# Six softmax exponentials and a transpose, issued half a slot earlier in an attention and soft-MoE kernel

## The chip, the cores and the metric

The kernel runs on one core of a Trainium2 chip. The metric is device time in microseconds. Before the change the median of three runs is 294.74 us (294.28 to 294.95).

## The reference, cut to what matters

Attention over 8 batches, 12 heads, 448 tokens and head dimension 64, with a one more in the denominator than softmax has (the term `exp(-m)`); then a soft mixture of experts over all 3584 tokens: 32 slots (8 experts of 4), each slot an average of the tokens (softmax down the tokens, "dispatch"), two dense layers, and each token a mixture of the slots (softmax along the slots, "combine").

```python
scores = scale * np.matmul(q, k.transpose(0, 1, 3, 2))
e = np.exp(scores - m)                              # m: maximum of the row
x = (e / (e.sum(-1) + np.exp(-m) + 1e-09)) @ v      # then 3584 x 768
logits = x @ phi                                    # 3584 x 32
d = softmax(logits, axis=0); slot_input = d.T @ x
c = softmax(logits, axis=1)
out = c @ experts(slot_input)
```

## The kernel before, in words

The kernel is written out by hand: each engine runs its instructions in the order of the program, and waits on semaphores of the others. The attention runs over 48 pairs of heads (six to a batch). The main loop (L766) has one **slot** s for a pair, in two halves, y = 0 and y = 1. In a slot the engines do this, for different pairs ahead of and behind s:

- Scores for the row maxima: PE L308 into PSUM (`ps_a`, pool psA of 3 buffers), DVE L309 reduces each one (617 ns); a last, shorter one is L325 and L327.
- Scores again, transposed, with the maxima added as a bias by a second matmul: PE L368 and L371 (`ps_b`, pool psB of 4 buffers), ACT L373 takes the exponentials; the shorter last one is L397, L400 and L403.
- The product with v, L437, twelve matmuls in each half and eight more in y = 0 (`ps_av`, one buffer); ACT L450 copies it out; DVE L468 adds up the denominator and L474 inverts it; POOL L478, L488 and L489 multiply.
- PX (L503): x of pair s-2 is turned by PE L510 into `ps_x` (psB), and ACT L516 casts it to xT. This is at the end of y = 1.
- The turns of q and k six slots ahead (L282, `ps_t` in psB and psA), copied out by ACT L286 (or DVE L286) and DVE L287. Every third slot the maxima are turned (`ps_m`) and copied by ACT L343 to `mT`.
- POOL also issues most loads (q: L176, k: L179, v: L183 and L184, expert weights: L113), and copies v into shape (V: L409 to L412, every third slot).

When a batch b is through the attention, its logits and both softmaxes are worked in between, in six steps that `P(b)` (L525) returns; each batch from the second on also rescales the sums of those before it by `corr`. The steps run in chosen halves of later slots: `post` (L672) maps a half slot 2s+y to what is issued there, after that half's AV matmuls and ahead of PX. For batches 0 to 5 (`late`, L521) with base half slot 2(6b+8):

- step 0: logits (L544), copy (L567), maximum (L571); step 1: transpose (L579), maximum (L581), `c_sub` on POOL (L586); step 2: new maximum (L592, L594) and `d_sub` on POOL (L600). These are in half slots 0, 1 and 2.
- step 3: `exps` on ACT (L605) out of `z` that `c_sub` and `d_sub` wrote, and `corr`: an exponential on ACT (L610) and the rescaling of `acc` on POOL (L616); batch 0 has no L610 and L616.
- step 4: `c_turn`, the combine weights turned by PE (L636, into `ps_ct` of psA) and copied by DVE (L637).
- step 5: `s_mm` and `s_add` (L632, L641), the dispatch sums.

Before the change steps 3, 4 and 5 are in half slots 4, 5 and 9. The half slots 2 and 3 are those of slot 6b+9, called the cast's slot in the prediction, whose L516 is the cast in question; 4 and 5 are those of slot 6b+10.

Of the kernel before, what the change touches and what calls it, by code (L numbers as in the profile page):

```python
# [31 lines left out]
def kernel(  # L32
# [123 lines left out]
    with ExitStack() as at:  # L156
# [364 lines left out]
        late = lambda b: b < B - 2  # L521
# [150 lines left out]
        post = {}  # L672
        for b in range(B - 1):
            for z, f in enumerate(P(b)):
                at_z = (0, 1, 2, 4, 5, 9) if late(b) else (0, 1, 2, 3, 4, 6)
                post.setdefault(2 * (PB * b + PB + 2) + at_z[z], []).append(f)

        ub = ubuf.rearrange("p n c -> p (n c)").bitcast(BF16)
# [371 lines left out]
```

## Time and profile before

| | |
|---|---|
| median of 3 runs | 294.74 us |
| profiled execution | 293.25 us |
| its span (first to last instruction) | 291.5 us |
| mean granted TensorE clock | 0.959 |
| step 3 to step 3, batches 3 to 4 and 4 to 5 | 28.23 us |
| DMA | 58.67 MB, 201 GB/s over the span |

A line of a timeline reads: start in us, length in us, engine, line of the kernel, operation, tile written <- tiles read, shapes, and how many instructions are merged. An entry in brackets is the idle time of the engine before it and what ended it. ACT's and DVE's records overlap by some 0.1 us when the engine is fed without a gap, so what an instruction costs is the time from its start to the next one's. A line of the page's groups reads: line, engine, operation, tiles, count | busy us, mean ns | idle before it and what ended most of it.

The attention's main loop fills the span from 60 to 236 us; the last batch, the experts and the output follow.

### The profile page before, as it was taken

Reading aid. Unit: us, or ns where it says so; the run is one execution under the profiler, and the core shown is the slowest. Engines: PE = TensorE matmul, PEld = TensorE weight load, DVE = VectorE, ACT = ScalarE, POOL = GpSimd, SP = SyncE. Lnnn points to the kernel's source line nnn. Section 1 sums busy time; section 2 is a strip of 40 time slices with the busy share of each in tenths; the row PEclk is TensorE's granted clock in tenths of the full one; section 3 lists DMA queues with packets and bytes.
Section 4 is the critical chain, followed back from the end, with each engine's and each line's share of the span. In section 5 each row is a group of like instructions: output and inputs, shape, how many; then the busy total and the mean of one; then the engine's idle time right before and its main releaser. Section 6 shows DMA issues by size and latency. Waiting matters only on the chain.

```text
span 291.5 us, 12388 instructions
## 1 busy us (share of the span) xinstructions
PE 266.0 (91%) x5191; PEld 153.7 (53%) x5191; DVE 248.2 (85%) x604; ACT 249.1 (85%) x555; POOL 189.6 (65%) x349
## 2 busy tenths in 40 slices
PE   5999899999999989999999999999999999996820
PEld 4545555555665545656655665566555556662100
DVE  5999899999999988999999999999999575437940
ACT  4569999999999989999999999999999987337820
POOL 8672897878787988798779878996785633000000
PEclk9999999999999999999999999999999999998555
DMA  8999999999999999999999999999999989908997
GB/s 144 144 151 208 143 139 166 201 169 198 183 187 182 197 172 203 159 185 177 202 196 194 173 201 184 195 180 204 147 135 205 216 190 261 345 6 325 409 447 331
DMA packets 47223, 58.67 MB, mean 201 GB/s; under 512 B 3008, under 2 KB 40128, under 8 KB 46912
## 3 DMA queue, kind: packets, MB, share of 16 engines
q0 software_dynamic: 40512, 42.29, 91.4%
q1 hardware_dynamic: 6656, 15.60, 13.8%
q8 instruction: 40, 0.66, 0.8%
q14 instruction: 15, 0.12, 0.1%
HBM read 89.16 MB, written 15.14 MB: 358 GB/s over the span
## 4 chain that ended last, share of the span: by engine, by line
PE 56%; ACT 16%; DVE 14%; issue 5%; DMA 3%; POOL 1%; DVEq 0%; POOLq 0%; ACTq 0%
PE ps_av L437 12%; PE ps_a L308 8%; DVE W L309 7%; ACT W L373 6%; PE ps_b L368 6%; PE ps_b L371 5%; ACT W L403 3%; PE ps_b L397 3%; PE ps_o L943 3%; PE ps_t L282 2%; ACT W L516 2%; PE ps_x L510 2%; DVE W L319 2%; PE ps_s L632 2%; PE ps_h L880 2%
## 5 line engine op out<-in xcount | busy, mean ns | idle before, releaser
L309 DVE TENSOR_REDUCE W<-ps_a 128x1 bf16<-128x448 f32 x250 | 138.8, 617 | 3.9 <-PE ps_a L308 2.4
L373 ACT ACTIVATE W<-ps_b 128x448 bf16<-128x448 f32 x250 | 122.2, 598 | 0.8 <-PE ps_b L371 0.8
L308 PE MATMUL ps_a<-W 64*128 64x448 bf16 x250 | 80.1, 352 | 0.0
L368 PE MATMUL ps_b<-W 64*128 64x448 bf16 x250 | 70.2, 352 | 1.2
L437 PEld LDWEIGHTS <-W 128*128 128x128 bf16 (+1 forms) x1536 | 50.4, 100 | 32.2 <-issue 29.4
L437 PE MATMUL ps_av<-W 128*128 128x65 bf16 (+1 forms) x1536 | 64.9, 196 | 1.5 <-issue 0.8
L371 PE MATMUL ps_b<-mT,sel 64*128 64x448 bf16 x250 | 64.8, 350 | 0.5 <-issue 0.5
L478 POOL TENSOR_TENSOR W<-ubuf,rec 128x384 bf16<-128x384 f32 x44 | 36.1, 821 | 35.2 <-DVE rec L474 24.8
L403 ACT ACTIVATE W<-ps_b 128x448 bf16<-128x448 f32 x86 | 47.9, 595 | 2.7 <-PE ps_b L400 2.6
L516 ACT CAST W<-ps_x 128x512 bf16<-128x512 f32 x47 | 30.2, 643 | 3.2 <-PE ps_x L510 2.2
L327 DVE TENSOR_REDUCE W<-ps_a 128x1 bf16<-128x448 f32 x48 | 29.6, 616 | 0.7 <-PE ps_a L325 0.7
L371 PEld LDWEIGHTS <-sel 64*128 64x128 bf16 x250 | 19.6, 94 | 16.9 <-issue 8.2
L113 POOL DMA_DIRECT2D W<-in_moe_w_dram x30 | 22.7, 757 | 8.1 <-PE ps_b L400 7.9
L308 PEld LDWEIGHTS <-W 64*128 64x128 bf16 x250 | 22.8, 94 | 9.6 <-issue 0.5
L397 PE MATMUL ps_b<-W 64*64 64x448 bf16 (+1 forms) x134 | 26.6, 366 | 0.2
L450 ACT COPY ubuf<-ps_av 128x455 f32<-128x455 f32 x44 | 25.7, 585 | 0.2
L400 PE MATMUL ps_b<-mT,sel 64*64 64x448 bf16 (+1 forms) x134 | 25.8, 364 | 0.1
L319 DVE TENSOR_REDUCE W<-ps_a 128x1 bf16<-128x448 f32 x38 | 21.1, 616 | 1.5 <-PE ps_a L316 1.4
L282 PEld LDWEIGHTS <-W 64*64 64x64 bf16 x1092 | 14.7, 108 | 13.2 <-issue 10.9
L489 POOL TENSOR_TENSOR W<-ubuf,rec 128x128 bf16<-128x128 f32 x44 | 17.5, 398 | 3.7
L510 PE MATMUL ps_x<-ident,W 128*128 128x128 bf16 x192 | 18.9, 219 | 0.8 <-issue 0.6
L325 PE MATMUL ps_a<-W 64*64 64x448 bf16 x96 | 18.7, 379 | 0.4
(154 smaller groups left out, 458.2 us busy)
## 6 DMA issues: line engine op xcount, KB each, us to landing
W<-in_moe_w_dram POOLq DMA_DIRECT2D x24, 768.0 KB, 9.3
W<-in_v_dram POOLq DMA_DIRECT2D x32, 192.0 KB, 6.0
out_dram<-W SPq DMA_DIRECT2D x2, 2688.0 KB, 9.1
W<-in_q_dram POOLq DMA_DIRECT2D x15, 336.0 KB, 6.2
W<-in_k_dram POOLq DMA_DIRECT2D x26, 168.0 KB, 6.4
stage<-in_moe_w_dram POOLq DMA_DIRECT2D x4, 768.0 KB, 9.6
W<-stage SPq DMA_DIRECT2D x4, 576.0 KB, 6.5
out_dram<-W SPq DMA_DIRECT2D x6, 384.0 KB, 2.7
```

Source lines behind the costliest of these rows:

```text
L308: nc.tensor.matmul(ps[:, 0:S], t[r, 0, qcs(hl, i)], t[r, 1, :], start=True, stop=True)
L309: nc.vector.reduce_max(mcol(n, i, hl), ps[:, 0:S], axis=AX.X)
L319: nc.vector.reduce_max(mcol(n, i, hl), pss[hl][:, 0:S], axis=AX.X)
L327: nc.vector.reduce_max(mcol(n, 3), ps[:, 0:S], axis=AX.X)
L368: nc.tensor.matmul(pss[hl][:, 0:S], t[rs[hl], 1, cols], t[rs[hl], 0, :], start=True, stop=False)
L371: nc.tensor.matmul(pss[hl][:, 0:S], sel[rs[hl], pl:pl + 1].to_broadcast([64, 128]), mT[mg(n)][rs[hl], 64 - 64 * hl:64 - 64 * hl + S], star ...
L373: nc.scalar.activation(e[:, hl, :], pss[hl][:, 0:S], AF.Exp, scale=scale)
L397: nc.tensor.matmul(outs[hl], t[rs[hl], 1, cols], t[rs[hl], 0, :], start=True, stop=False)
L403: nc.scalar.activation(e, p[:, 0:S], AF.Exp, scale=scale)
L437: nc.tensor.matmul(o, eT[n, i, hl][:, qcs(hl, u)], vp[g % 2][:, 2 * pl + hl, i, 0:W65], start=(i == 0 and u == 0 and hl == 0) or (u == 3 a ...
L478: eng.tensor_mul(x[:, 0:3, c:c + 128].rearrange("p i (h d) -> p i h d", h=2), u[:, 0:6, 0:D].rearrange("p (i h) d -> p i h d", h=2), rec[: ...
L516: nc.scalar.copy(xT(b, pb), pss[0])
```

## The change

One list is changed: the half slots of the six steps for batches 0 to 5. Step 3 goes from half slot 4 to 3, step 4 from 5 to 4.

```diff
             for z, f in enumerate(P(b)):
-                at_z = (0, 1, 2, 4, 5, 9) if late(b) else (0, 1, 2, 3, 4, 6)
+                at_z = (0, 1, 2, 3, 4, 9) if late(b) else (0, 1, 2, 3, 4, 6)
                 post.setdefault(2 * (PB * b + PB + 2) + at_z[z], []).append(f)
```

In the order of instructions on each engine, six times over:

- ACT: L605 and L610 come ahead of the cast L516 of slot 6b+9; before, they came behind it and the four L373 after it, ahead of L450.
- PE: L636 comes between the AV matmuls of slot 6b+10's first half (behind the first twelve, ahead of the eight); before, it came behind those of the second half, ahead of PX.
- DVE: L637 comes behind the fourth of slot 6b+10's six L309; before, behind the L474 after the sixth.
- POOL (batches 1 to 5): L616 comes ahead of L409 to L412 and the loads of v, L183 and L184; before, behind them.
- SP: unchanged.

## The prediction, made before the result was known

> **What bounds the kernel now.** I read the page's first part, then the waits and the chain, then the timeline of ACT, DVE, POOL and PE around the six places that the diff moves.
>
> ```profile
> PE 266.0 (91%) x5191; PEld 153.7 (53%) x5191; DVE 248.2 (85%) x604; ACT 249.1 (85%) x555; POOL 189.6 (65%) x349
> ...
> L516 ACT CAST W<-ps_x 128x512 bf16<-128x512 f32 x47 | 30.2, 643 | 3.2 <-PE ps_x L510 2.2
> ```
>
> No engine alone is the bound: PE, DVE and ACT are each full in the attention (60 to 236 us). I added up what each engine stands beyond the closest spacing of the same two lines: about 12 us on ACT and 13.5 on DVE between 60 and 236 us, and 0.9 to 1.0 us of it on ACT in each of batches 3 and 4. From exponential L605 to the next batch's L605 it is 28.23 us for batches 3, 4 and 5 (154.16, 182.39, 210.62). So the question is which engine's delay the others feel. The timelines of batch 2 (first ACT, then DVE, then POOL; start, length in us) carry the sum:
>
> ```profile
> 122.66 0.58 ACT L403 ACTIVATE W<-ps_b 128x448 bf16<-128x448 f32 x1
> 123.23 0.59 ACT L516 CAST W<-ps_x 128x512 bf16<-128x512 f32 x1
> 123.72 1.85 ACT L373 ACTIVATE W<-ps_b 128x448 bf16<-128x448 f32 x4
> 125.44 0.44 ACT L605 ACTIVATE cd<-z 128x256 bf16<-128x256 f32 x1
> 125.74 0.25 ACT L610 ACTIVATE corr<-z 128x32 f32<-128x32 f32 x1
> 125.86 0.56 ACT L450 COPY ubuf<-ps_av 128x455 f32<-128x455 f32 x1
> ```
>
> ```profile
> 122.51 0.42 DVE L468 SCALAR_TENSOR_TENSOR rec<-ubuf,ec 128x7 f32<-128x7 f32 x1
> ...
> 126.94 0.30 DVE L468 SCALAR_TENSOR_TENSOR rec<-ubuf,ec 128x7 f32<-128x7 f32 x1
> 127.16 0.38 DVE L287 COPY W<-ps_t 128x448 bf16<-128x448 bf16 x1
> ...
> 128.10 0.17 DVE L637 COPY cT<-ps_ct 128x128 bf16<-128x128 bf16 x1
> ```
>
> ```profile
> 122.36 0.54 POOL L600 TENSOR_TENSOR z<-lb,lb 128x160 f32<-128x160 f32 x1
> ...
> 125.20 0.40 POOL L489 TENSOR_TENSOR W<-ubuf,rec 128x128 bf16<-128x128 f32 x1
> 125.55 0.66 POOL L409 COPY W<-W 128x576 bf16<-128x576 bf16 x1
> 126.27 0.66 POOL L410 COPY W<-W 128x576 bf16<-128x576 bf16 x1
> 126.88 0.34 POOL L411 COPY W<-W 64x192 bf16<-64x192 bf16 x1
> ...
> 129.02 0.66 POOL L616 TENSOR_TENSOR acc<-acc,corr 128x224 f32<-128x224 f32 x1
> ```
>
> See three things: ACT starts each instruction before the last record ends, so its cost is start to start; DVE's seven-element L468, usually 0.156 us, takes 0.42 and 0.30 here, ending as the POOL instruction begun before it ends; and L600, which makes the exponentials' input, ends (122.90) only just before ACT could want it.
>
> **The change, step by step.** Nothing is added or removed; by the order of instructions on each engine, five things move, and their waits with them.
>
> *ACT: L605 and L610 ahead of the cast L516.* They cost 125.86-125.44 = 0.42 us where they are (0.30 in batch 0, which has no L610). At the new place ACT stands today: an L403 with a ready cast behind it takes 0.44 (127.55 to 127.99), here 0.57, so 0.13 is a wait for PX. The cast thus moves by 0.42-0.13 = 0.29, and the copy L450, four exponentials on, comes 0.13 earlier, if its input is there. PE's AV matmuls end at 125.48, with L636 among them 0.06 later; L450 follows that end by 0.15 elsewhere (120.69 to 120.84), so it may start at 125.69. ACT is there at 125.73. Gain 0.13 on ACT, kept.
>
> *The wait that this adds.* L605 waits for L600 on POOL; queued behind it on ACT are the cast and the four exponentials, and PE's next score waits for that cast's buffer (L368 starts at 123.82, as the cast ends). L605 can start 0.44 after L403 starts; against the end of L600 the room is 64.43-64.16 = 0.27 (batch 0), 93.06-93.69 = **-0.63 (batch 1)**, 123.10-122.90 = 0.20, 151.82-151.12 = 0.70, 180.05-179.86 = 0.19, 208.28-207.32 = 0.96. Today four exponentials (1.7 us) cover it. Batch 1 is late because POOL issued its loads late (here POOL, then ACT):
>
> ```profile
> 91.06 0.82 POOL L176 DMA_DIRECT2D W<-in_q_dram  x1 [0.77 <-PE ps_a L308]
> 91.89 1.25 POOL L179 DMA_DIRECT2D W<-in_k_dram  x2
> 93.16 0.53 POOL L600 TENSOR_TENSOR z<-lb,lb 128x160 f32<-128x160 f32 x1
> ```
>
> ```profile
> 92.62 0.58 ACT L403 ACTIVATE W<-ps_b 128x448 bf16<-128x448 f32 x1
> 93.20 0.59 ACT L516 CAST W<-ps_x 128x512 bf16<-128x512 f32 x1
> ```
>
> There L605 starts at 93.73, the cast at 93.73+0.42 = 94.15 for 93.20, and L450 at 94.15+0.49+1.72 = 96.36 for 95.83 (0.49 and 1.72 are the starts 123.23, 123.72 and 125.44): +0.5. PE and DVE are pulled along by the late buffer. I take +0.55; below, 0: PE stands 0.85 at 101.9 and 0.55 at 108.7 for nothing that the profile names, which could swallow it; above, +0.8, DVE's own share.
>
> *Batch 0.* PE stands 0.58 inside PX, so the cast waits till 65.07 in any case and the exponential's 0.30 vanishes in that wait. But the copy of the weights' turn, L637, now comes between PE's turns of q and k and their buffer: they slip by 0.2. I take -0.1, bounds -0.3 and 0.
>
> *POOL: L616 moves ahead of the copies L409 to L412 and the two loads of v.* Its 0.62 (129.02 to 129.64) only changes place; POOL is at L478 at 129.64 as before. The loads of v start 0.62 later; they take 6.0 us by the page's part 6 and serve the head pairs three slots (14 us) on: nothing. L616 waits for L610, done by 124, and POOL reaches it at 125.55: nothing.
>
> *What that does to DVE.* L409 now starts at 125.55+0.62 = 126.17 and L410 0.72 later, 126.89 to 127.55: a 0.66 copy where the 0.34 one, L411, lay. L468 comes at 126.94 plus 0.09 (L637 now ahead of it; 128.10 to 128.19). It is held till about 127.57, and L287 starts at 127.50 for 127.16: +0.33. L637 no longer stands behind it: -0.09. DVE enters the next slot 0.24 late. The same sum for the others: L410 at 97.30, 155.34, 183.84 and 211.80, L468 at 97.5 (behind batch 1's stall), 155.53, 183.99 and 212.00: held each time. Batch 0 has no L616. Bounds: 0, if L468 gets in first as at 96.69 today (0.156 beside an L410 that began in the same instant); 0.5, the whole of L410.
>
> The Trainium skill, "SBUF — State Buffer", section "SBUF: two separate sides", states that a DVE instruction with two SBUF inputs and a GpSimd one that reads SBUF exclude each other for a whole instruction, the first comer winning. The trace agrees (122.51 held to 122.93 behind an L600 that ends at 122.90). By the rule this change is charged for a copy that it does not touch; without it the DVE step would be zero and the sum about -0.1 (-0.1+0.55-4x0.13).
>
> *Does the delay reach the end?* In batch 3, DVE runs 0.27 earlier than in batches 2 and 4 (its L468 in the cast's slot is not held) and merely stands 0.25 in the next slot (158.24 to 159.02, against 0.53); the period is 28.23 all the same. So 0.25 is free in batches 3 and 5 (there 215.48), but already spent in 2 and 4, whose DVE has no idle time till about 0.1 at 133.26. For batch 2 I carried the 0.24 on: the score that waits for a reduce goes from 128.90 to 129.09, L450 from 130.16 to 130.2, DVE's copy of q's turn, L286, from 132.09 to 132.33; the scores behind it wait for that copy and their bias matmuls for mT's copy on ACT, so that the reduce at 133.26 starts at 133.46. So +0.2 for batches 2 and 4, and their 0.13 is lost. Batches 3 and 5 keep 0.1 and 0.05 of theirs.
>
> *PE: L636 half a slot earlier.* Its 0.06 is moved; it takes a psA buffer one round earlier, so the last two scores of that half wait one reduce more (0.06 and 0.2), which is in the carried sums.
>
> Sum, batches 0 to 5: -0.1 +0.55 +0.2 -0.1 +0.2 -0.05 = **+0.7 us**. The profiled execution is 293.25 (span 291.5 and 1.75 around it), 1.5 below the median of the runs shown; the step is a difference, so I add it to the median: 294.74+0.7 = 295.4.
>
> **The rivals.**
> 1. *Nothing to be seen.* Batch 1's stall is swallowed by PE's two nameless gaps, and 2 and 4 lose only what 3 and 5 gain: -0.1+0+0.2-0.1+0.2-0.05 = +0.15, so 294.9. For it: each engine has idle time somewhere. Against: PE's gaps may simply move along. 0.28.
> 2. *Faster.* The 0.13 before the cast is filled in five batches and batch 0 gives 0.3: -0.95, so 293.8. Its mechanism is ACT's wait before the cast, filled with work that had to be done anyway; it decides as soon as L600 is done before L403 is through and L468 reaches DVE ahead of L410, that is 0.14 to 0.2 earlier than I put it. For it: of the six late loads on POOL only batch 1's happened (0.77). Against: the held L468 of today. 0.15.
> 3. *Much slower.* The room of 0.20 and 0.19 in batches 2 and 4 is used up by a DVE that is 0.2 late at the maxima that L600 waits for, so these stall as batch 1 does: 0.7+2x0.55 = +1.8, so 296.5. Against: at every third slot the engines meet again at mT's copy, which takes most of such a lag off. 0.12.
>
> **The numbers.** My forecast (+0.6 to +1.2) has 0.45. I count 0.2% (0.6 us) as what a measurement of this kernel can tell from no change. Slower: 0.45+0.12 = 0.57; same 0.28; faster 0.15. The range runs from most of the second rival, 293.9, to beyond the third, 296.9.
>
> **What would show it.** In the changed profile L605 stands before L516 with no wait in batches 2 to 5 and some 0.6 us behind L600 in batch 1; the cast starts 0.86 after L403; L468 in the slot behind takes 0.4 to 0.6 us in five places; DVE's idle time at the fifth reduce of batches 3 and 5 is gone; L605 to L605 is 28.2 to 28.5. I am wrong if L468 stays at 0.16, if batch 1's L600 comes in time, or if the periods shorten by 0.13.

## The result, and the profile after

The changed kernel takes 296.9 us (median of 16 runs, 293.75 to 298.36) beside 294.02 us for the kernel before in the same session (16 runs): 1.0078 times, 95% interval 1.0051 to 1.0105. (The ratios leave out runs more than 1.5% above the fastest of their kernel, here two of each, so 1.0078 is not 296.9 over 294.02.) Two later sessions gave 1.0014 (0.9977 to 1.0052) and 1.0048 (1.0015 to 1.0082). Weighted by the inverse squares of their half-widths the three make 1.0054: **slower, by about 1.6 us**. The size is less certain than each interval says: the sessions give 2.3, 0.4 and 1.4 us, which lie further apart than their intervals allow for, and the second is not clear of no change. The forecast was slower by 0.7.

The profiled execution is 294.65 us, span 292.9, against 293.25 and 291.5. Busy times are those of before within 1 us:

```profile
PE 265.5 (91%) x5191; PEld 154.0 (53%) x5191; DVE 248.7 (85%) x604; ACT 249.5 (85%) x555; POOL 189.7 (65%) x349
...
L368 PE MATMUL ps_b<-W 64*128 64x448 bf16 x250 | 70.0, 353 | 1.4 <-ACT W L516 0.7
...
L516 ACT CAST W<-ps_x 128x512 bf16<-128x512 f32 x47 | 29.7, 633 | 3.3 <-PE ps_x L510 2.5
```

New is what stands at the end of the second line: PE's scores wait 0.7 us in all for the cast L516, which is one wait in batch 1, shown below. The same place of batch 2 as before the change, on ACT:

```profile
123.15 0.58 ACT L403 ACTIVATE W<-ps_b 128x448 bf16<-128x448 f32 x1
123.59 0.45 ACT L605 ACTIVATE cd<-z 128x256 bf16<-128x256 f32 x1
123.90 0.26 ACT L610 ACTIVATE corr<-z 128x32 f32<-128x32 f32 x1
124.02 0.61 ACT L516 CAST W<-ps_x 128x512 bf16<-128x512 f32 x1
124.48 1.90 ACT L373 ACTIVATE W<-ps_b 128x448 bf16<-128x448 f32 x4
126.19 0.62 ACT L450 COPY ubuf<-ps_av 128x455 f32<-128x455 f32 x1
```

L605 starts 0.44 behind L403, with no wait; the cast comes 0.87 behind L403 (0.57 before), and L450 3.04 (3.20 before): the wait ahead of the cast is filled, and ACT is 0.16 ahead. On DVE and POOL, a little later:

```profile
127.56 0.50 DVE L468 SCALAR_TENSOR_TENSOR rec<-ubuf,ec 128x7 f32<-128x7 f32 x1
127.98 0.38 DVE L287 COPY W<-ps_t 128x448 bf16<-128x448 bf16 x1
```

```profile
126.05 0.66 POOL L616 TENSOR_TENSOR acc<-acc,corr 128x224 f32<-128x224 f32 x1
126.65 0.66 POOL L409 COPY W<-W 128x576 bf16<-128x576 bf16 x1
127.38 0.66 POOL L410 COPY W<-W 128x576 bf16<-128x576 bf16 x1
127.98 0.35 POOL L411 COPY W<-W 64x192 bf16<-64x192 bf16 x1
```

L616 now lies ahead of the copies, L468 comes into L410 (127.38 to 128.04) and is held till 128.06; before, it met L411 and lost 0.15. And in batch 1 (ACT, POOL, PE):

```profile
94.36 0.58 ACT L403 ACTIVATE W<-ps_b 128x448 bf16<-128x448 f32 x1
95.45 0.42 ACT L605 ACTIVATE cd<-z 128x256 bf16<-128x256 f32 x1 [0.51 <-POOL z L600]
95.78 0.21 ACT L610 ACTIVATE corr<-z 128x32 f32<-128x32 f32 x1
95.90 0.57 ACT L516 CAST W<-ps_x 128x512 bf16<-128x512 f32 x1
```

```profile
92.79 0.82 POOL L176 DMA_DIRECT2D W<-in_q_dram  x1 [0.76 <-PE ps_a L308]
93.62 1.25 POOL L179 DMA_DIRECT2D W<-in_k_dram  x2
94.89 0.53 POOL L600 TENSOR_TENSOR z<-lb,lb 128x160 f32<-128x160 f32 x1
```

```profile
96.51 0.35 PE L368 MATMUL ps_b<-W 64*128 64x448 bf16 x1 [0.75 <-ACT W L516]
```

L605 starts 1.09 behind L403 where it is 0.44 in batch 2, just after L600 ends, and PE stands 0.75 for the cast's buffer.

**Where the time lies.** I cut each trace at the casts L516 of slots 6b+8 and 6b+12: six stretches that hold all that the change moves. Their lengths in us, from the starts of L516 in the timelines ("between them" goes on to the last cast, 23.0 us behind the sixth stretch; what is left of the span behind that is 46.2 to 46.3 us in each):

| kernel | b 0 | 1 | 2 | 3 | 4 | 5 | up to the first | between them |
|---|---|---|---|---|---|---|---|---|
| before | 19.19 | 19.71 | 18.79 | 18.74 | 18.79 | 18.56 | 59.89 | 71.61 |
| before, again | 18.79 | 18.93 | 18.79 | 18.74 | 18.79 | 18.80 | 61.55 | 73.65 |
| changed | 18.80 | 19.35 | 18.90 | 18.66 | 18.92 | 18.61 | 60.80 | 72.65 |
| changed, again | 19.06 | 19.36 | 18.92 | 18.66 | 18.93 | 18.88 | 60.51 | 71.18 |
| changed, third | 18.76 | 19.35 | 18.91 | 18.69 | 18.92 | 18.61 | 61.16 | 71.44 |
| batch 1 alone | 19.07 | 19.36 | 18.79 | 18.75 | 18.79 | 18.79 | 61.28 | 71.92 |
| hold alone | 19.21 | 18.90 | 19.05 | 18.74 | 19.06 | 18.50 | 61.20 | 70.88 |
| step 3 alone | 19.15 | 19.50 | 19.05 | 18.74 | 19.06 | 18.50 | 61.18 | 71.63 |
| corr old | 18.55 | 19.31 | 18.69 | 18.66 | 18.69 | 18.45 | 61.07 | 72.82 |
| batch 1 old | 18.87 | 18.90 | 18.92 | 18.66 | 18.92 | 18.45 | 61.28 | 71.78 |
| corr and batch 1 old | 18.76 | 18.97 | 18.69 | 18.66 | 18.69 | 18.60 | 60.25 | 72.17 |

Batches 2 to 4 repeat to 0.03 us. Batches 0, 1 and 5 hold gaps of PE that the profile puts down to nothing (0.2 to 0.8 us in batch 0, 0.85 in the first kernel's batch 1, 0 to 0.6 in batch 5) and are compared where these are alike: batch 0, 18.76 beside 18.79 with gaps of 0.31 and 0.22, so about -0.1; batch 1, 19.35 beside 18.93, +0.4; batch 5, 18.61 beside 18.80 with gaps of 0.33 each, -0.2 (without gaps 18.45 in "batch 1 old" beside 18.56, -0.1). With +0.12, -0.07 and +0.13 for batches 2, 3 and 4 the stretches sum to +0.3 or +0.4 us. The columns to the right scatter by more than 1 us between executions, though no instruction there is in another order.

### The profile page after: what moved, and what is told of

The parts are those of the page before. It is cut to its first block, busy times and chain, and to the rows that moved or that the text cites. A ratio compares the mean times of both kernels' runs of the same rounds, so it can differ in the third digit from the quotient of the medians.

```text
span 292.9 us, 12388 instructions
## 1 busy us (share of the span) xinstructions
PE 265.5 (91%) x5191; PEld 154.0 (53%) x5191; DVE 248.7 (85%) x604; ACT 249.5 (85%) x555; POOL 189.7 (65%) x349
## 4 chain that ended last, share of the span: by engine, by line
PE 63%; ACT 12%; DVE 11%; issue 4%; DMA 3%; POOL 2%; DVEq 0%; POOLq 0%; ACTq 0%
PE ps_av L437 14%; PE ps_a L308 9%; PE ps_b L368 7%; PE ps_b L371 6%; DVE W L309 5%; PE ps_b L397 4%; DMA W<-in_k_dram 3%; PE ps_t L282 3%; ACT W L373 3%; PE ps_x L510 3%; ACT W L403 3%; PE ps_o L943 2%; DVE W L319 2%; PE ps_s L632 2%; PE ps_h L880 2%
## 5 line engine op out<-in xcount | busy, mean ns | idle before, releaser
L309 DVE TENSOR_REDUCE W<-ps_a 128x1 bf16<-128x448 f32 x250 | 138.4, 616 | 3.9 <-PE ps_a L308 3.1
L373 ACT ACTIVATE W<-ps_b 128x448 bf16<-128x448 f32 x250 | 122.1, 596 | 0.5 <-PE ps_b L371 0.5
L308 PE MATMUL ps_a<-W 64*128 64x448 bf16 x250 | 81.3, 351 | 0.2
L403 ACT ACTIVATE W<-ps_b 128x448 bf16<-128x448 f32 x86 | 47.3, 588 | 2.8 <-PE ps_b L400 2.6
L516 ACT CAST W<-ps_x 128x512 bf16<-128x512 f32 x47 | 29.7, 633 | 3.3 <-PE ps_x L510 2.5
L308 PEld LDWEIGHTS <-W 64*128 64x128 bf16 x250 | 23.2, 93 | 9.5
L450 ACT COPY ubuf<-ps_av 128x455 f32<-128x455 f32 x44 | 25.7, 583 | 0.2
L282 PEld LDWEIGHTS <-W 64*64 64x64 bf16 x1092 | 14.7, 108 | 14.1 <-issue 10.9
L510 PE MATMUL ps_x<-ident,W 128*128 128x128 bf16 x192 | 18.9, 219 | 1.8 <-ACT W L403 1.1
L489 POOL TENSOR_TENSOR W<-ubuf,rec 128x128 bf16<-128x128 f32 x44 | 17.6, 399 | 3.7
```

The source lines that it names most:

```text
L308: nc.tensor.matmul(ps[:, 0:S], t[r, 0, qcs(hl, i)], t[r, 1, :], start=True, stop=True)
L309: nc.vector.reduce_max(mcol(n, i, hl), ps[:, 0:S], axis=AX.X)
L373: nc.scalar.activation(e[:, hl, :], pss[hl][:, 0:S], AF.Exp, scale=scale)
L403: nc.scalar.activation(e, p[:, 0:S], AF.Exp, scale=scale)
L510: nc.tensor.matmul(pss[i // 2 if two else 0][:, o:o + 128], x[:, i, c], ident if i < 3 else ident2, start=True, stop=True)
L516: nc.scalar.copy(xT(b, pb), pss[0])
```

## The experiments

Two theories of mine and a rival. **Z**: ACT stands before L605 for z, above all in batch 1. **H**: L468 is held behind L410. My forecast was their sum, less what ACT gains. **P**: PE stands for nothing named, and more often than before. Each ratio is to the kernel before in the same session.

**The changed kernel again** (no edit).

> The changed kernel once more, unchanged. All theories: 1.005 to 1.010 times the kernel before. In its profile, theory Z (late z: ACT stands before L605 for L600 on POOL, in more or other batches than batch 1) expects waits of 0.3 us or more before L605, which add up to most of the loss of 2 us; theory H (hold: L468 behind L410) expects no wait before L605 but L468 of 0.45 to 0.5 us in four batches and a loss of 0.2 us in each; theory P (PE stands for nothing that the profile names, and more often than before) expects the loss in those gaps.

1.0014 (0.9977 to 1.0052), below what all three theories expected. L605 starts 0.66 us late in batch 1 and nowhere else; L468 takes 0.48, 0.51, 0.39 and 0.51 in batches 1 to 4. So Z does not spread to other batches, which speaks against a large Z and against the prediction's third rival: the room ahead of L605 is 0.19 and 0.18 in batches 2 and 4, as before the change.

**Step 3 alone early.**

```diff
-at_z = (0, 1, 2, 3, 4, 9) if late(b) else ...
+at_z = (0, 1, 2, 3, 5, 9) if late(b) else ...
```

> Step 3 half a slot early as in the changed kernel, step 4 (the weights' turn) back in its old place. Theory Z: as slow as the changed kernel (1.007), the wait before L605 stays. Theory H: L468 comes 0.09 us earlier, still inside L410, so about 0.1 us a batch is won: 1.005. If the early turn on PE, with its psA buffer, is the cause instead: 1.000.

1.003 (1.0005 to 1.0056). The time alone decides nothing here: the changed kernel itself stood at 1.0014 in the same session, well inside each other's intervals. The trace says more: with the turn L636 back in its old place the stretches of batches 1, 2 and 4 are longer than in the changed kernel, not shorter, so the early turn is not what costs time there. H's number for this run was wrong in sign: L468 arrives 0.09 earlier, meets more of L410 and is held longer (0.64 in batches 2 and 4), and those stretches are 19.05 and 19.06 for 18.9. The early turn, by delaying L468, spares part of the hold.

**Corr left in its old half slot.**

```diff
-both(exps, corr)] + ([c_turn, both(s_mm, s_add)] if late(b) else ...
+*([exps, corr, c_turn, both(s_mm, s_add)] if late(b) else ...)]
-at_z = (0, 1, 2, 3, 4, 9) if late(b) else ...
+at_z = (0, 1, 2, 3, 4, 4, 9) if late(b) else ...
```

> As the changed kernel, but corr (ACT L610 and POOL's rescaling L616) stays in the old half slot, so POOL's order is the old one and L468 meets the short copy L411 or nothing. Theory H: the loss goes, 1.000 to 1.002, and L468 is back to 0.16 to 0.3 us. Theory Z: the loss stays, 1.006, for L605 still waits for L600. Theory P: 1.007.

1.0038 (1.0005 to 1.0072). In the trace H is borne out; DVE, then POOL of batch 2:

```profile
126.98 0.17 DVE L468 SCALAR_TENSOR_TENSOR rec<-ubuf,ec 128x7 f32<-128x7 f32 x1
```

```profile
126.18 0.66 POOL L410 COPY W<-W 128x576 bf16<-128x576 bf16 x1
126.78 0.34 POOL L411 COPY W<-W 64x192 bf16<-64x192 bf16 x1
```

POOL's order is the old one, L468 meets L411 near its end, and batches 2 and 4 are 18.69: 0.1 less than before the change, where ACT's filled wait now shows. Batch 1 keeps its wait (L605 at 94.91, 0.52 idle) and its 19.31. So both mechanisms are there and separate. The time was expected at 1.000 to 1.002 by H and does not say how much of the loss H was: it is no lower than the 1.0014 of the changed kernel beside it.

**The loads of q and k issued behind d_sub.**

```diff
-            if s > 2 and s + 2 in firsts:
+            if s > 2 and (s + 2 in firsts or s % 6 == 2 and s < 44):
                 wait_loads.append((slot_loads, s))
```

> As the changed kernel, but POOL issues the loads of q and k of slot 6b+8 behind d_sub (L600) instead of ahead of it, in batches 0 to 4, so z is ready 1 us or more before ACT wants it. Theory Z: the loss goes, 0.998 to 1.001, and no wait before L605. Theory H: about 1.003, for L468 is still held, by whatever of POOL's copies it then meets. Theory P: 1.007.

1.0033 (1.0006 to 1.006). z is ready 0.9 us or more before L605 in each batch, and no wait is left there; but POOL comes later to x, and in batch 1 PE stands for it instead:

```profile
103.67 0.34 PE L510 MATMUL ps_x<-ident,W 128*128 128x128 bf16 x3 [0.27 <-POOL W L478]
104.43 0.23 PE L510 MATMUL ps_x<-ident,W 128*128 128x128 bf16 x1 [0.41 <-POOL W L489]
```

That stretch is 19.91. The wait was moved, not removed; as a test of Z it settles nothing.

**Batch 1 as before, the rest changed.**

```diff
-at_z = (0, 1, 2, 3, 4, 9) if late(b) else ...
+at_z = ((0, 1, 2, 4, 5, 9) if b == 1 else (0, 1, 2, 3, 4, 9)) if late(b) else ...
```

> The changed kernel with batch 1 alone as before. Sum theory: batch 1's 0.6 us comes back, the rest (plus 0.1 in batches 2 and 4, less in the others) is next to nothing: 0.6 us faster than the changed kernel, 0.999 to 1.001 of before; no wait before L605. Theory P: as the changed kernel.

1.0021 (0.9993 to 1.005), above the 0.999 to 1.001 expected, which the interval still holds. It is 0.0033 below the changed kernel's pooled 1.0054, but no run of the changed kernel was made beside it, so that difference stands on weak ground. No wait before L605; batch 1 is 18.90.

**Both undone: corr old, and batch 1 as before.**

```diff
-at_z = (0, 1, 2, 3, 4, 4, 9) if late(b) else ...
+at_z = ((0, 1, 2, 4, 4, 5, 9) if b == 1 else (0, 1, 2, 3, 4, 4, 9)) if late(b) else ...
```

It is the third experiment's kernel with this edit.

> Exponentials and weights' turn half a slot early, but corr (L610, L616) in its old half slot, and batch 1 wholly as before. By the profile of the kernel with corr alone put back, batches 2 to 5 take about 0.1 us less than before (18.69, 18.66, 18.69, 18.45 for 18.79, 18.74, 18.79, 18.56 from cast to cast over four slots), so the sum theory (batch 1's wait for z plus the held L468) expects 0.998 to 0.999 times the kernel before, a gain of 0.4 to 0.7 us. If something else that no step names costs the time (theory P: PE's nameless gaps), 1.003 as the kernels with the early step 3 had.

1.0003 (0.9975 to 1.0031). The stretches are as short as expected. The time shows no loss, and no gain either: the interval holds the 0.998 to 0.999 expected as well as a loss of 0.9 us, so a version that beats both isn't shown.

**Batch 1 alone changed.**

```diff
-at_z = (0, 1, 2, 4, 5, 9) if late(b) else ...
+at_z = ((0, 1, 2, 3, 4, 9) if b == 1 else (0, 1, 2, 4, 5, 9)) if late(b) else ...
```

> The kernel before with batch 1 alone changed. Sum theory: all that the change costs is here: 1.002 (0.6 us), L605 of batch 1 waits 0.65 us for L600 and that stretch is 19.35 where it was 18.7; the other five as before. If the loss lies in the other batches: 1.000.

1.0029 (0.9999 to 1.0058). The wait is there once more:

```profile
94.31 0.58 ACT L403 ACTIVATE W<-ps_b 128x448 bf16<-128x448 f32 x1
95.41 0.42 ACT L605 ACTIVATE cd<-z 128x256 bf16<-128x256 f32 x1 [0.53 <-POOL z L600]
```

The stretch is 19.36; batches 2 to 4 are those of before.

**The hold alone** (the kernel before, with corr half a slot early in batches 2 to 5).

```diff
-both(exps, corr)] + ([c_turn, both(s_mm, s_add)] if late(b) else ...
+*([exps, corr, c_turn, both(s_mm, s_add)] if late(b) else ...)]
-at_z = (0, 1, 2, 4, 5, 9) if late(b) else ...
+at_z = (0, 1, 2, 4, 3 + (b == 1), 5, 9) if late(b) else ...
```

> The kernel before, but in batches 2 to 5 the short exponential L610 and POOL's rescaling L616 come half a slot earlier; the long exponential L605 and the weights' turn stay, and batches 0 and 1 are as before. Theory H: L468 of the slot behind meets the 0.66 copy L410 and takes 0.55 to 0.65 us (L637 does not delay it here) where it took 0.3 and 0.25; the slot after it is 0.2 to 0.3 us longer in batches 2 and 4 and 0 to 0.1 in 3 and 5; in all 0.2 to 0.6 us, 1.001 to 1.002. If L468 gets in first in these places, stretches and time are as before.

1.0048 (1.0015 to 1.0082), for 1.001 to 1.002 expected. L468 in batch 2, DVE, then POOL:

```profile
126.71 0.64 DVE L468 SCALAR_TENSOR_TENSOR rec<-ubuf,ec 128x7 f32<-128x7 f32 x1
127.27 0.38 DVE L287 COPY W<-ps_t 128x448 bf16<-128x448 bf16 x1
```

```profile
126.66 0.66 POOL L410 COPY W<-W 128x576 bf16<-128x576 bf16 x1
```

The stretches of batches 2 and 4 grow by 0.26 and 0.27, those of 3 and 5 not: the same DVE delay is free where DVE had idle time and counts where it had none. The time, 0.4 to 2.4 us longer, just holds the 0.5 us of the stretches at its lower end.

**The kernel before against itself.**

> The kernel before against itself: 1.000. It tells how much two equal kernels differ in one session and in where their profiles spend time: the sum theory expects the six stretches (cast of slot 6b+8 to cast of slot 6b+12) at 18.8, 18.7, 18.8, 18.7, 18.8, 18.6 us wherever PE does not stand for nothing named, and the time up to the first of them to scatter by some 1 us from execution to execution, as it does between kernels that are the same up to there (59.9 to 61.3).

0.9986 (0.9949 to 1.0023). Its stretches are those that the theory gave, but for batch 1 (18.93 for 18.7, with no gap of PE's to explain it) and batch 5 (a gap of 0.33), and the rest of its span is 3.7 us longer than in the first profile of the same kernel (61.55+73.65 for 59.89+71.61).

**The changed kernel a third time.**

> The changed kernel a third time. Sum theory: 1.002 to 1.004 (0.6 to 1.0 us), as forecast, and the 1.0078 and the 1.0014 of the two sessions so far are scatter around it; stretches of 18.8, 19.35, 18.9, 18.66, 18.92, 18.5. Theory P, that the change makes stalls likelier outside its own stretches: 1.006 or more, and the stretches as above.

1.0048 (1.0015 to 1.0082), between the two predictions; stretches as both expected.

**z made later by 1 us**, in the changed kernel and in the one before: d_sub done three times over, with the same values.

```diff
-                eng.tensor_sub(...)
+                [eng.tensor_sub(...) for _ in range(3 if late(b) else 1)]
```

> The changed kernel with d_sub done three times over on POOL in batches 0 to 5 (same values), which makes z some 1.0 us later. If ACT's cover of four exponentials is what the change gave away, L605 now stands in batches 0 to 4: about 1.6 us in batch 1, 0.7 to 0.8 in batches 2 and 4, 0.3 in batch 3, 0.2 in batch 0 behind PE's own gap, none in 5; 2.5 to 4 us slower than the changed kernel, 1.010 to 1.016 of before.

> The kernel before with the same threefold d_sub. Four exponentials (1.7 us) cover the later z, so no wait before L605 but at most 0.3 us in batch 1 (room today 1.7 us); what is left is POOL's own 1.0 us and a longer hold of L468: 1.000 to 1.003 of before. If it is as slow as the changed kernel with the same delay, the cover is not what counts.

1.0164 (1.0118 to 1.021) and 1.0076 (1.0041 to 1.011), the first at the upper end of what was expected, the second above it. In the changed kernel with the later z, this ended the idle time ahead of L605 (us in total, times), and this waited for the casts L516:

```profile
  POOL z L600: 4.5, 5
```

```profile
  PE ps_b L368: 4.8, 5
```

Its stretches of batches 1 to 4 are 21.76, 19.75, 19.11 and 19.77: 2.4, 0.8, 0.4 and 0.8 us more than in the changed kernel. In the kernel before, no L605 waits for L600, not even in batch 1, where L600 ends at 98.86 and L605 starts at 99.36; the stretches are 18.79, 18.75 and 18.79 in batches 2 to 4, as without the delay, and 19.59 in batch 1, where PE waits 0.42 us for POOL's x (L489). So what stood ahead of L605, the cast and the four exponentials, was a cover. It was worth 2.3 us (123.10 to 125.44 in batch 2), not only the 1.7 of the exponentials that I counted. Between the two kernels with the delay lie 0.0088 of the time before, some 2.6 us in one session. The 1.0076 was not expected and stays open: in both profiles with the delay the time up to the first stretch is the longest of all (62.79 and 63.31 us), though no instruction there differs, and two executions don't account for the timed runs.

## Why the prediction was right, and where it was not

- *The cast 0.29 later, L450 0.13 earlier.* Right: 0.30 and 0.16.
- *The wait for z.* Right in place and size: batch 1 alone, L605 0.65 us late in all three profiles of the changed kernel. L450 comes 3.70 behind L403 for 3.20, the +0.5 forecast; the stretch is +0.4 for the 0.55 forecast, so its slots behind that win some 0.1 back. The timed runs give 0.0029 with batch 1 alone, and 0.0033 less with it undone: 0.9 and 1.0 us, each +-0.9 or more, the second across sessions.
- *PE's two nameless gaps* (the lower bound, and the first rival). The 0.85 and 0.55 us stand in the first profile of the kernel before and in no other, so no profile shows whether they could swallow the stall. Against that first profile alone batch 1 would look shorter after the change, 19.35 for 19.71.
- *The hold of L468.* Right in mechanism and size where forecast: 0.50 and 0.51 in batches 2 and 4 for the 0.54 that the working gives (127.03 to 127.57). It let L287 start 0.36 late against its closest spacing, 0.15 before. The Trainium skill's rule ("SBUF — State Buffer", section "SBUF: two separate sides"), the first comer has the shared ports for its whole instruction, fits: L468 ends at 128.06, L410 at 128.04. L468 got in ahead of L410, as the second rival needs, in none of batches 1 to 5 of the three profiles. In batch 5 it takes 0.21 to 0.32, not the some 0.48 of the working (212.00 to the end of L410), where PE's gap of 0.3 to 0.6 ahead of it brings L468 to the end of L410; without that gap 0.40.
- *Free in batches 3 and 5, dear in 2 and 4.* Right in sign: -0.07 and -0.2, +0.12 and +0.13 for the +0.2 forecast. The 0.25 us that DVE stood at the fifth reduce is gone in batch 3 and 0 to 0.08 in batch 5. Batches 2 and 4 are 0.2 late at the cast of slot 6b+11, as I carried on, but the slot behind it takes 4.91 us for 5.00 and gives 0.1 back.
- *Batch 0.* -0.1, as forecast.
- *L600 late in more batches* (the third rival): no; the room stayed 0.19 to 0.22 in batches 2 and 4.
- *The period.* I put L605 to L605 at 28.2 to 28.5 us. For batches 2 to 5 it is 28.2 to 29.3 in the three profiles, and 28.2 to 29.4 in the second profile of the kernel before: what lies between the stretches moves more than the change does.
- **The sum.** The stretches give +0.3 or +0.4 for 0.7, the timed runs about 1.6. So the direction and the two mechanisms were right, and the size was not: it lies between what the traces show and what the clock shows. The 296.9 us of the first session is the very end of my range, which reached that far for the third rival, and that did not happen; that the number lies in the range is in part luck. The term that was mis-sized is the one I put at zero without naming it: what happens outside the six stretches.
- **What stays open.** Undoing batch 1, the early corr, or both leaves 1.0021, 1.0038 and 1.0003; either alone costs 1.0029 and 1.0048. That order fits two causes, but the intervals (+-0.003) overlap, and 1.0021 and 1.0048 belong to kernels with much the same hold; it is no proof that the whole 1.6 us is theirs. Some 1 us stays open. Theory P is neither shown nor ruled out for it. The profiles at hand speak against it rather than for it: PE's gaps of 0.2 us and more for which the profile names nothing sum to 2.3 and 1.9 us between 60 and 236 us in the two profiles of the kernel before, and to 1.2, 1.7 and 0.6 in the three of the changed one, and those three executions (294.65, 293.48 and 293.8 us) are not slower than those two (293.25 and 296.01). The time up to the first stretch and between the stretches moves by 1 to 3 us among profiles in which those parts are the same, so one profile of a kernel can't settle it.

## What to carry to other kernels

Before moving an instruction ahead in a full in-order queue, write down when its input is ready and when the queue would reach it, for each repetition: here five of six had room, some by only 0.2 us, and by the stretches the sixth cost 0.4, more than the move won in any of the others. What stood between producer and consumer was cover, not delay; a test that makes the producer later, in both kernels, shows its worth. And follow everything that moves along: the rescaling on POOL, which nobody waited for, pushed a longer copy under a seven-element instruction of DVE.

## What the runs showed of the hardware

- A DVE instruction of seven elements with two inputs in SBUF took 0.64 us when it came 0.05 us behind the start of a 0.66 us copy on POOL, 0.50 us when it came 0.18 us behind it, and 0.15 to 0.17 where nothing held it; the delay depends on where in the copy it falls.
- POOL stood 0.75 to 0.77 us ahead of the load L176 of batch 1 in every profile in which that load keeps its place, before and after the change, 0.99 where it was put behind d_sub, and less than 0.1 ahead of every other L176 from 60 us on. The prediction took it for chance. The profile puts it down to PE's L308; no run shows whether that is its cause.
- PE stood 0.2 to 1.0 us with no wait that the profile names, often at the same places of the program (L510 at 65 to 66, L282 at 145 to 149 and at 207 to 210 us), in lengths that differ from execution to execution.
